# Loading the q of an attention block in one transfer and its k in two, with the whole order of instructions drawn again

## The chip, the cores and the metric

The kernel runs on one core of a Trainium2 chip. The metric is the device time of one execution in microseconds (us). Before the change it is 675.41 us (median of three runs, 675.41 to 675.98).

## What is computed

A transformer block on 2048 tokens (S) of width 448 (D), in float32: layer norm, attention with 16 heads of 28 channels in which each token sees itself and the 255 tokens ahead of it, a residual, layer norm, a GEGLU feed-forward part with 1792 hidden channels, and a residual.

```python
qkv = (x @ wqkv).reshape(B, S, 3, H, Dh)             # H = 16, Dh = 28
scores = einsum("bhqd,bhkd->bhqk", q, k) * Dh ** -0.5
mask = (idx[:, None] - idx[None, :] >= 0) & (idx[:, None] - idx[None, :] < 256)
p = softmax(where(mask, scores, -1e9))
o = einsum("bhqk,bhkd->bhqd", p, v)                  # then @ wo
h = x + A(layernorm(x))
h2 = h + (gelu(n @ w_gate) * (n @ w_up)) @ w_down    # n = layernorm(h)
```

## The kernel before, in words

**Numbers.** Most operands are kept as two or three parts of lower precision, a high part and what is left of it, and a product is a sum of several matmuls over such parts. ScalarE (ACT) writes high parts (L252), VectorE (DVE) or GpSimd (POOL) the low ones (L255), and `mul` (L249) is the one line of nearly all matmuls on TensorE (PE).

**Stages.** First x is loaded in 16 tiles of 128 tokens (L510), normalised, and transposed on PE (L320). `project_tile` makes 128 rows of q or k for a chunk of 512 tokens with eleven matmuls of 512 columns; ACT and DVE split the sum into parts in SBUF, and `put` stores them to DRAM with two DMAs (L656 two parts, L657 one part). The heads form four groups of four (112 channels each); there are two passes p of two groups. The k of the last group is made from 16 rows left over in each of seven tiles, so it goes to DRAM in small pieces (16 rows).

**Attention blocks.** A block B is one group g and one chunk c of 512 tokens: 16 blocks, eight in each pass, c = (B % 8) // 2. `loads(B)` brings q and k back from DRAM in another layout: the 84 rows are 28 channels in three parts, and four heads stand side by side. One tile is 128 tokens of four heads. A block needs four tiles of q, and of k the same four and the two of the chunk ahead (for c = 0 there are none). Each `get` (L678) loads two tiles, 336 KB: a block with c > 0 issues five (k of the chunk ahead, then q, k, q, k), one with c = 0 issues four. The buffers for q and k are two, used by turns (u = B % 2), so a load of block B can be issued only when the matmuls of block B-2 that read the same two tiles have ended.

`scores` multiplies q with k (up to 384 columns) and DVE takes the maximum (L701); `maxima` splits the maxima (DVE L721), transposes them on PE (L728) and has ACT copy them beside q, so that `probs` makes the scores again with the maxima taken off; ACT does exp (L775) and POOL cuts the mask (L788, select). `attend` multiplies with v (L807), `drain` divides by the sums (L830 to L835), `output` multiplies with wo (operands wos, ohl).

**What sets the order.** The program builds a list of operations, each with its engine, costs and a key, and a table PLAN of numbers plays them: it fixes the order on every engine, on SyncE (SP) too, which issues all DMAs in order, and the PSUM banks. A DMA at the head of SP that waits for its data or its buffer holds all behind it. Transposes of `ident` (L1315) fill gaps of PE. The feed-forward part follows from about 306 us on.

Of the kernel before, what the change touches and what calls it, by code (L numbers as in the profile page):

```python
# [135 lines left out]
def block_kernel(ctx: ExitStack, tc, x, wqk_in, wv_in, wo_in, ffn_in, halves_in, out):  # L136
# [499 lines left out]
    def project_tile(p, c, m):  # L636
# [17 lines left out]

        def put(rows, d, name, s, size):
            dma(key, 458 * size, lambda: nc.sync.dma_start(d[:, s:s + 2], both[rows]), tok, [(name, 0)])  # L656
            dma(key, 229 * size, lambda: nc.sync.dma_start(d[:, 2 - 2 * s], both[rows, 0]), tok[0:1], [(name, 1)])  # L657
        put(slice(0, GF), qk_d[g][c][s], ("d", g, s, c), s, 1)
        put(slice(GF, 128), qk_d[NG - 1][c][1][16 * m:16 * m + 16], ("d", NG - 1, 1, c, m), 1, 0.15)
# [8 lines left out]
    def loads(B):  # L668
        g, c = block(B)
        u = B % 2  # L670

        def get(s, cc, lo, n, at, key):
            src = qk_d[g][cc][s].rearrange("(j p) b t -> (p b) j t", j=4)[:, :, lo * 128:(lo + n) * 128]
            dst, tok = (rk, "rk") if s else (rq, "rq")
            rd = [(("d", g, 1, cc, m), i) for m in range(WT) for i in range(2)] if s and g == NG - 1 else \
                [(("d", g, s, cc), i) for i in range(2)]
# [1 line left out]
            dma(key, 246 * n, lambda: nc.sync.dma_start(f(dst[u][0:3 * DH, :, at * 128:(at + n) * 128]), src),  # L678
                rd, [(tok, u, at + i) for i in range(n)])
# [646 lines left out]
    "{i7-vjspMgN*MO#VNOw4-TbdwSR_Z_KlOoOB=B!c{<jt=%o_X8YUr=mAJ+b;6@||v9Nvrnvz!00{_kl5|LzJHRws(oKaM<ycsO$qd8V<jZcyYX"
    "4Obh4D~rQx|LX_C=>9zs{vAQ#)9|11fBXL5{r>lL|Nq7Pzw^T&VT2VY!ipWqNUTWxr-<;?K}wJfq>7l49T*@!hzC-G#2^Yt4|0V5PoFd(CddUc"
    "fM_5GNCq;3v>*iX01qSq=|J-T%*_j;gPb5L$OLkO%Ag9!2daW<zz5Yq4WNLUAT!7hl7bi@%YWvy1_eMH&=#}<?Lh~S6$sD~bOHq<JUWA!unQ;z"
    "x`JAuHmCzk&<)fD^+93K0H~lL2tXsy7&HM*K{L=CXrKis0a}8=U<hahro*8i5s+XQhzo{;5nu+K1((2)U=)}QM}sk78LS7!0t-w5-N8~g6&QFN"
    "=mDmIB49e0180EoU?!La955Tq0TVz^Fc+2urNE>JRCB>{I1$)j9#{ZZz@=arFmW#s4bKP5L2s}EBmjNDLbwRbg9|`$uq0x}N-!U;0xRJ{&=;%*"  # L1330
    "YrrDd4{QS#?hm$u0bnCs1#P?-o&*wS53L1j;U;(*tOEmq3wD6La5Y>HqT|hQAM8!m!9k!H*a>3b^>9B-igtnBz`>`$7PtZK0Y$+9xESmO`@mK>"
    "8SDpZ;5K*woB`XRi(}%xgd-2f!VjT>0(=mDf<E2>Kf|5yAov1z!LP6nsRa6w4d5FbL3YFM@Fd&=AHhT56nqT(lSA+{+z3MWFc4@nh=LEpA8->m"
    "0)N8TxFm>*kHRD12|Na$!ZYw0EDerB6`h4A;B%NBzkui9OL!i>f*0UxcoAL%aquPZ29^UEa7O$K#>bc7d#Ite@G|@jGvO<+JkZfQco|dxFF<B|"
    "1!Rd3{V0+ZR|E#S3a^7~cr?k56W|*l5rpU^_z15-6UD_>!3TI9TBr=T2BM(&Fb9r@ZL}5KfKNa|92Mon(GWs6VJ>_NJ^};CZ5SPmBu~K|h>=8N"
    "$Xyr%Jq85bgE3Jed>_U_x4{E=9t<Q7x&v;4S6~pi0AeE_-2#>I5K;xd1{5X6RdEtLn1oO@TpcHdXTeZ%4lwivxab2IOOAm!s0O|Z-hu?MCLTtT"
    ";#xQ%{0NfaxM&=?2Zj?5b;aXJHyohk_&BJICz2F69-2T>;&&hw?vCT5)c6^A57OWyuntaw(&GDI5=ns4;Vs|+sEeP2qo4<Ff**o}C^P&7GQytt"
    "GZ=}oz@)Gjo=ke<OfV%(jQZeIuqmEGzJO-<8z=y?!oIi&EC|1XemFPIgNwqvI3KQu^W*Oz8*GjX;NPGz{sHRa{+LD_*NM<iP!Q*Xzd%D=2)Drb"
    "VN1+l16&w$SPC}6MX&-PEDc-Xq8LF9o&c?}fI74whBj=2lOq+j#RLXW!ge?WOF$Dwf$gyaU04zp$0cw{Y(Ni|!ck!t+yR%yWpFfD7N>{FkPpk@"
    "@;C#mfQ#W|up&+i3&H5H5>5w;!Opl0EDSs1>@YPPfQ!QzuoEr|hvGD_988JI!yGUL$_XpLTyPj3h%3S2I5!-DW5SWRA{>lI;Z$fU$pc5@)MyMI"
    "f~S#mC@+i!)1bF>I!TYl;@Ge`Ob%PX86+*L569t_a3&dqv!Pj}0jv(QquFE*sS0brxnv&6fvUmzWIWD^YQhDiGR%N#!3j7M%807KqvROLjE<9u"  # L1340
    "xG}5?+rcLA1et`}!z`#C>;O-atf(VAMLNNTuq?`j3Zl`d6>J1^quQ`FJWUFrQRob51J9DqupF9-^PtjbA<2uzpmU@dEQ5-oMPwRYO!A?^s2HjP"
    "myoe&DantDpk-t^X$z;|6=Wr;g$khaWHN3FtDveV4lIsVk=p12NdZ@rlBfi#hN`2uunR1OYM_fG9$Z7}pz^2!>Ix^Iif9~KODdylq#LY@>Y?#y"
    "9l1^_q3&=xzCk9U^<)FNMCzlPWFu*eHjy513Tl8hlP0Jm+CpxTsi+g`infw&Xf?V`x}$Am4Vr|ulRIQGT8eg%IjASROO~P5s0Zqa=AwI~4eAB&"
    "lLw?1+KAes-tZyWg!;gSs5fek+M&Mi5$Ok8plPTkYL6PB{%|@P06U;rs3{r=XQMu7CT@mC!Oo~J8VE<j8Mq%B16!j0=qg!>W}pFR5bT1kkX2|f"
    "90H$_nP@#~g%+c=Xcis{2cmgsEL?(~kmYC?91iEB%VZrI2N$40Xa!n?HlTNOA=-?_!!2k8d`f2HC3q{E0GHy4a68(8R^Y*CCz=Gep?zpSnhaOs"
    "DewTA3U{IBWE#ATmf=Ns2-=NakmdL#*@K3nS7b4MO|GCj=q@^nPNI8gFM30Up*i?1IfmYmxp)CSg$|-a=sj78hocYVH{OUplEdgG+JtwK-S`u^"
    "g?5qMWDj12Z=*frH2O;RlFwux*-y@(tLQPgj}DN7WHo+Icj80jI68t3lWS-f{y{FH6X+-TK!1@V<UHDp&!S7{LBz%5A)1FTphxH&`b{92AMr?f"
    "j3B*%wqQiI;wNZ7Msy9v<T~1hG5tvQ;_Y}Xeu@aCbO&a11X_pp;b(}`19$^Ih(FQw_z+g8MxUd@_&g@$DE>w-V4axc1^P^nVM;FI<M;%AiB4jR"
    "9Ki}P$SHgVpT)1xLu}A<SS6>iO$5~lBd^hQ{EZ0m2&?ohdV?gnf#0F`s3iYRIr)GbqSNT)3%!Y5@&#SOukdSp3&$WI(I@l<U&S8ziaw*u_!@qU"
    "zoD=6Ilh9wqZjxGdV+t@pXew3jb7rI<SzEf9ef|hinwk=Y|#h!Eq;f8A%yQ?lfK9C$!+`rCnO2TM~pGUHhqRaVS*D8jwMy_Q%teIUr1~cmwd)i"  # L1350
    "NgR@xs93}CNI<^eC?pAqMt;!{NlJA5n<gV)aX^!kJuC%DMM5+NO--WFG$bZXN%pd|BnpjA_px*&1Ib9DQitwmnMh8Op13qK@n|lRg&bf$%}(0V"
    "tRyAPO}>+ZEC)$N)6z;L52;M5kaV;vNlr_XYNQPLh7Yk6G!Ffa%aX$^E=^67(!3-MJ;Jh)f+QbFOq0>0tPm+q3XmkUFgeCbkfP)Vu1?C4BBVTt"
    "McdP}tQg5p&av3E9X-z~kPECMEk!P}c=QrG&Mvd~v?95}e&Va_47<iklIyGk%}CSJ8!Q3ML~D?QGy}cO64A^w3q8Sp;hXF<%SvmKTPz>#L9^2w"
    "G(SBV@%VwP7p+CI(NhdD%yQD&q&Foj7p1HK%}smK%9OD#G!NxWVReXLMQIhPvVt@(y~n!JVzdyw&oow&K469EL^_@pr;}(Y`j8c&k5~yhfsUn*"
    "SzS_^j-yrSR9c4ip-<Q}T8~tt<>^z_mp)?^Xhk}i)}$X;C0dI%pylWkI-1s|4QV6Vn2w<XXm$FWHKBFrKw6jfqh)D*@}AYB4M>05jecZJX(!r{"
# [155 lines left out]
```

## Time and profile before

| | |
|---|---|
| median of three runs | 675.41 us |
| the profiled execution's own time | 675.42 us |
| its span in the trace | 673.7 us |
| busy: PE, DVE, ACT, POOL | 662.4, 511.0, 406.9, 325.1 us |
| matmuls in the trace | 4074 |
| loads of q and of k (L678) | 32 and 44, of 336 KB each |
| granted clock of PE | 1.0 |

How to read the views: times are us from the span's start. A row of the timeline or of the chain of waits has the start, the length, and the engine, line and operation; "bank<-ring" is output<-input by the program's names, with numbers left out, and xN says how many instructions are drawn together. SPq is SP issuing a DMA. PEld is the loading of a matmul's weights, which runs beside the matmul ahead of it. In the order of instructions (from the program and not from a run), rows stand in issue order on one engine, with the output's and the input's names and the shape.

### The profile page before, as it was taken

Reading aid. Unit: us, or ns where it says so; the run is one execution under the profiler, and the core shown is the slowest. Engines: PE = TensorE matmul, PEld = TensorE weight load, DVE = VectorE, ACT = ScalarE, POOL = GpSimd, SP = SyncE. Lnnn points to the kernel's source line nnn. Section 1 sums busy time; section 2 is a strip of 40 time slices with the busy share of each in tenths; the row PEclk is TensorE's granted clock in tenths of the full one; section 3 lists DMA queues with packets and bytes.
Section 4 is the critical chain, followed back from the end, with each engine's and each line's share of the span. In section 5 each row is a group of like instructions: output and inputs, shape, how many; then the busy total and the mean of one; then the engine's idle time right before and its main releaser. Section 6 shows DMA issues by size and latency. Waiting matters only on the chain.

```text
span 673.7 us, 12051 instructions
## 1 busy us (share of the span) xinstructions
PE 662.4 (98%) x4074; PEld 591.8 (88%) x4074; DVE 511.0 (76%) x1287; ACT 406.9 (60%) x793; POOL 325.1 (48%) x506
## 2 busy tenths in 40 slices
...
GB/s 296 204 257 234 272 203 180 210 190 196 153 188 212 209 207 227 157 112 86 140 108 102 102 96 119 103 91 93 20 71 53 122 68 119 54 67 55 64 15 109
DMA packets 97814, 93.73 MB, mean 139 GB/s; under 512 B 39064, under 2 KB 86360, under 8 KB 97752
## 3 DMA queue, kind: packets, MB, share of 16 engines
...
q14 instruction: 30, 0.25, 0.1%
...
## 4 chain that ended last, share of the span: by engine, by line
PE 91%; DVE 3%; DMA 2%; SPq 1%; issue 1%; POOL 1%; ACT 1%; DVEq 0%; POOLq 0%
PE bank L249 84%; PE bank L807 6%; DVE bank L701 1%; DMA ring<-k 1%; DMA pp<-in_wv_dram 1%; DMA q<-proj 1%; POOL proj L255 1%; PE bank L320 1%; PE bank L728 0%; DVE mhl L721 0%; ACT pp L775 0%; SPq L657 0%; ACT ring L252 0%; POOL pp L788 0%; SPq L510 0%
## 5 line engine op out<-in xcount | busy, mean ns | idle before, releaser
L249 PE MATMUL bank<-xT,proj 128*128 128x512 f32 x648 | 183.4, 386 | 0.0
L701 DVE CUSTOM_DVE_ANT_0 bank<-bank,mask 128x384 f32<-128x384 f32 (+2 forms) x256 | 131.5, 550 | 23.5 <-PE bank L249 18.4
L249 PE MATMUL bank<-ring 84*128 84x384 f32 (+7 forms) x629 | 140.1, 311 | 1.7 <-DMA ring<-k 0.7
L249 PEld LDWEIGHTS bank<-xT,proj 128*128 128x128 f32 x648 | 118.5, 190 | 12.4 <-issue 0.4
L249 PE MATMUL bank<-xT,ring 128*128 128x512 f32 x508 | 127.5, 379 | 0.0
L249 PE MATMUL bank<-ring,proj 128*128 128x448 f32 x617 | 125.3, 353 | 0.0
L249 PEld LDWEIGHTS bank<-ring,proj 128*128 128x128 f32 x617 | 116.5, 189 | 2.8
L249 PEld LDWEIGHTS bank<-ring 128*128 128x128 f32 (+1 forms) x629 | 106.1, 190 | 12.5 <-ACT pp L775 2.0
L775 ACT ACTIVATE pp<-bank 128x384 f32<-128x384 f32 (+1 forms) x212 | 103.9, 534 | 21.8 <-PE bank L249 18.2
L249 PEld LDWEIGHTS bank<-xT,ring 128*128 128x128 f32 x508 | 95.9, 189 | 12.2 <-DVE v L1022 0.3
L788 POOL TENSOR_SCALAR_AFFINE_SELECT pp<-pp 128x512 f32<-128x512 f32 x120 | 73.3, 639 | 63.1 <-ACT pp L775 61.2
L249 PE MATMUL bank<-proj,xT 128*128 128x224 f32 x352 | 72.6, 268 | 1.1 <-ACT proj L252 1.1
L946 POOL TENSOR_TENSOR raw<-raw 64x128 f32<-64x128 f32 (+1 forms) x110 | 54.9, 510 | 28.7 <-DMA raw<-in_halves_dram 17.1
L249 PEld LDWEIGHTS bank<-proj,xT 128*128 128x128 f32 x352 | 59.4, 191 | 2.3 <-ACT proj L252 1.3
L255 POOL TENSOR_TENSOR ring<-raw,ring 128x256 fp32r<-128x256 f32 (+2 forms) x48 | 43.1, 906 | 35.1 <-ACT ring L252 34.2
L1022 DVE TENSOR_TENSOR v<-v,bank 128x512 f32<-128x512 f32 x48 | 32.8, 683 | 30.6 <-PE bank L249 26.0
L252 ACT ACTIVATE ring<-bank 8x512 fp32r<-8x512 f32 x64 | 37.0, 584 | 24.5 <-PE bank L728 23.6
L255 DVE TENSOR_TENSOR proj<-v,proj 128x512 fp32r<-128x512 f32 (+1 forms) x57 | 38.6, 691 | 17.3 <-ACT proj L252 17.0
L249 PE MATMUL bank<-wos,ohl 128*128 128x448 f32 x192 | 49.3, 359 | 0.1
L252 ACT ACTIVATE proj<-v 128x512 fp32r<-128x512 f32 (+1 forms) x57 | 32.9, 593 | 26.2 <-DVE v L1048 13.6
L1078 DVE TENSOR_TENSOR hres<-bank,hres 128x448 f32<-128x448 f32 x64 | 37.5, 616 | 12.7 <-PE bank L249 12.6
L946 POOL TENSOR_TENSOR v<-raw 128x256 f32<-128x256 f32 x22 | 18.0, 818 | 57.2 <-DMA raw<-in_halves_dram 30.1
...
## 6 DMA issues: line engine op xcount, KB each, us to landing
...
```

What stands on the lines that cost most here:

```text
L249: nc.tensor.matmul(o.rearrange("p (t h) -> p t h", h=2), w, mixed(m), **how)
L252: nc.scalar.activation(dst, src, AF.Copy)
L255: (eng or nc.vector).tensor_sub(dst, src, f(hi))
L320: nc.tensor.transpose(bank[b.k][:, n * 128:(n + 1) * 128], xn[i2][:, o:o + 128], ident)
L701: nc.vector.tensor_tensor_reduce(at, at, plain(mask[:, o:384]), 1.0, -BIG, OP.add, OP.max, mx[i // 2][:, i % 2, j:j + 1])
L775: nc.scalar.activation(pp[:, j:j + per, o * 128:o * 128 + n].rearrange("p j (h t) -> p j h t", h=2), bank[b.k][:, 0:n * per].rearrange("p ...
L788: nc.gpsimd.affine_select(a, a, pattern=[[0, 4], [-cm, 128]], compare_op=op_, fill=0.0, base=0, channel_multiplier=cm)
L807: nc.tensor.matmul(bank[b.k][32 * j:32 * j + DH + 1, lo * 128:(hi + 1) * 128], v[:, 4 * c - 2 + m, g % 2, j, :], pp[:, j, at[m] * 128:(at[ ...
L946: op("pool", 0.14 + n * 0.00215, 0.18 + n * 0.00215, key, lambda: nc.gpsimd.tensor_tensor(out, a, b, op=OP.subtract), [*ar, *br], w, port= ...
L1022: op("dve", 0.605, 0.702, key, lambda: nc.vector.tensor_tensor(plain(out), plain(a), unmixed(bank[bs[i].k]), op=OP.add), ar, w, bs[i])
L1078: op("dve", 0.533, 0.626, key + 3 * q + 3, lambda t=t, b=banks[q]: nc.vector.tensor_tensor(plain(hres[:, t, :]), unmixed(bank[b.k][:, 0:D] ...
```

## The change

In DRAM each group's q and k now is one tile over all 2048 tokens instead of four of 512, so a stored row of two parts falls into two runs of 2 KB where it was one of 4 KB. A block's q is loaded in one transfer of four tiles (672 KB). Its k is loaded, for c > 0, as the first four tiles (672 KB) and the last two (336 KB), and for c = 0 as four at once. That makes 44 loads instead of 76. The whole-q load waits for all of block B-2's matmuls that read that q.

```diff
+LOADS = {2: 492, 4: 560, 6: 760}
+ROWS = (((0, 0, 4, 0), (1, 0, 4, 0)), ((0, 0, 4, 0), (1, -2, 4, 0), (1, 2, 2, 8)))
...
-    qk_d = [[[dram.tile([GF, 3, 512], F32, name=f"{'qk'[i]}{g}_{c}") for i in range(2)] for c in range(CS)]
-            for g in range(NG)]
+    qk_d = [[dram.tile([GF, 3, S], F32, name=f"{'qk'[i]}{g}") for i in range(2)] for g in range(NG)]
...
-            dma(key, 458 * size, lambda: nc.sync.dma_start(d[:, s:s + 2], both[rows]), tok, [(name, 0)])
+            dma(key, 458 * size, lambda: nc.sync.dma_start(d[:, s:s + 2, at], both[rows]), tok, [(name, 0)])
...
-            dma(key, 246 * n, lambda: nc.sync.dma_start(f(dst[u][0:3 * DH, :, at * 128:(at + n) * 128]), src),
+            dma(key, LOADS[n], lambda: nc.sync.dma_start(f(dst[u][0:3 * DH, :, at * 128:(at + n) * 128]), src),
                 rd, [(tok, u, at + i) for i in range(n)])
         key = 16 * B - (8 if B > 1 else 24)
-        if c:
-            get(1, c - 1, 2, 2, 0, key)
-        for i in range(0, 4, 2):
-            get(0, c, i, 2, i, key + 4 * i)
-            get(1, c, i, 2, 2 + i, key + 4 * i)
+        for s, t, n, k in ROWS[c > 0]:
+            get(s, t, n, key + k)
...
 PLAN = (
-    "c-pOZW3+5L)McEV?QGSxZQHhO+qP}nwr$(CZ5w^wx%KY%`cIG1qkGh-IxES_%3O2J<Rl1C00992aKHeHXfc2zY!cazBCLOYQN%cout22EBP|f&"
...
+    "c-pPGW7H+f5-pm}tjaR-Ywosf+qP}nwr$(CZQHhOci%p}zrD}7|K1z#jT);~X5@^Fh#3*Ns>T9<0t5&E00Rd2pBeZ)BELuY_xwLH@MjhMzS!>%"
...
```

The table PLAN is replaced as a whole, so instructions move on every engine up to about 306 us; the feed-forward part keeps its order on PE. The numbers of matmuls, of DVE, ACT and POOL operations stay as they are, but for the transposes of `ident`, which are 33 instead of 30. Lines stand one (matmul, 249 to 250) to seven (load, 678 to 685) further down.

Three places. On SP, the start of the program (hres is x, raw the weights of q and k, pp the weights of v), before:

```order
L510 DMA hres<-in_x_dram 128x448 x4
L583 DMA pp<-in_wv_dram 128x448
L609 DMA raw<-in_wqk_dram 128x512
L583 DMA pp<-in_wv_dram 128x448
L510 DMA hres<-in_x_dram 128x448
L609 DMA raw<-in_wqk_dram 128x512
L510 DMA hres<-in_x_dram 128x448 x10
```

and now:

```order
L511 DMA hres<-in_x_dram 128x448 x3
L584 DMA pp<-in_wv_dram 128x448
L511 DMA hres<-in_x_dram 128x448
L584 DMA pp<-in_wv_dram 128x448
L511 DMA hres<-in_x_dram 128x448 x2
L610 DMA raw<-in_wqk_dram 128x512
L511 DMA hres<-in_x_dram 128x448 x2
L610 DMA raw<-in_wqk_dram 128x512
```

The second load of v's weights is the sixth DMA and was the seventh, with none of the weights of q and k ahead of it; those are the ninth and twelfth and were the sixth and ninth.

On SP, around the loads of block 1, whose q and k are those of group 1, chunk 0 (before q1_0 and k1_0, now q1 and k1; the last number is a buffer's), before:

```order
L657 DMA q1_1_96<-proj_78 112x512
L656 DMA k3_1_113<-proj_78 16x1024
L657 DMA k3_1_113<-proj_78 16x512
L860 DMA raw_79<-in_wo_dram 128x448
L657 DMA k3_1_113<-proj_78 16x512
L657 DMA k3_0_111<-pp_145 16x512
L678 DMA ring_77<-k1_0_95 84x4x256
L678 DMA ring_77<-q1_0_94 84x4x256
```

and now:

```order
L659 DMA k1_89<-pp_121 112x2x512
L660 DMA q0_86<-proj_78 112x512
L685 DMA ring_77<-q1_88 84x4x512
L660 DMA k0_87<-proj_78 112x512
L660 DMA k3_93<-proj_78 16x512
L659 DMA k3_93<-proj_78 16x2x512
L659 DMA q0_86<-proj_78 112x2x512
L685 DMA ring_77<-k1_89 84x4x512
```

The last load of block 1's k was the 55th DMA of the program and is the 44th now; it stood behind stores of chunk 1 of group 1 and of the last group, and stands behind those of chunk 1 of group 0 now.

On PE, in the middle, between the last matmul of block 3 that reads its q (the first row of each piece) and the first scores of block 5 (the last row; ring holds q and k). Rows with xT are of the projection, L728 or L732 is the transpose of the maxima, L807 or L811 the start of block 4's attend. Before:

```order
L249 MATMUL bank7_141<-ring_77 128x384
L249 MATMUL bank3_137<-ring_77 128x384
L249 MATMUL bank1_135<-ring_77 128x128 x2
...
L249 MATMUL bank2_136<-xT_76,proj_78 128x512 x3
L728 MATMUL bank1_135<-one_84,mhl2_150 72x128
L807 MATMUL bank5_139<-pp_145,v_81 29x128 x4
...
L728 MATMUL bank0_134<-one_84,mhl0_148 72x128
L249 MATMUL bank1_135<-ring_77 128x256
L249 MATMUL bank6_140<-ring_77 128x384
```

and now:

```order
L250 MATMUL bank3_113<-ring_77 128x128
L250 MATMUL bank0_110<-xT_76,proj_78 128x512
L250 MATMUL bank7_117<-ring_77 128x384
L250 MATMUL bank6_116<-ring_77 128x384
L250 MATMUL bank1_111<-ring_77 128x384
L250 MATMUL bank0_110<-xT_76,proj_78 128x512 x4
L250 MATMUL bank7_117<-ring_77 128x384
L250 MATMUL bank2_112<-ring_77 128x384
L732 MATMUL bank3_113<-one_84,mhl2_126 72x128
...
L732 MATMUL bank1_111<-one_84,mhl0_124 72x128
L250 MATMUL bank7_117<-ring_77 128x384
```

The 24 matmuls of attend stand between them in both. Beside those there were 21 matmuls from the release of block 3's first two q tiles to the first scores of block 5, and there are 12 now from the release of all four.

More of the change, by code (lines that the diff above doesn't have):

```diff
@@ L652, in project_tile @@
         op("dve", 0.603, 0.698, key, lambda: to_lo(plain(hl[1]), unmixed(bank[b.k]), plain(hl[0])), [tok[0]], [tok[1]], b)
+        at = slice(512 * c, 512 * c + 512)
         def put(rows, d, name, s, size):
[L656 to L659, printed above, removed]
+            dma(key, 458 * size, lambda: nc.sync.dma_start(d[:, s:s + 2, at], both[rows]), tok, [(name, 0)])
+            dma(key, 229 * size, lambda: nc.sync.dma_start(d[:, 2 - 2 * s, at], both[rows, 0]), tok[0:1], [(name, 1)])
+        put(slice(0, GF), qk_d[g][s], ("d", g, s, c), s, 1)
+        put(slice(GF, 128), qk_d[NG - 1][1][16 * m:16 * m + 16], ("d", NG - 1, 1, c, m), 1, 0.15)
     def block(B):
@@ L670, in loads, with get @@
         u = B % 2
-        def get(s, cc, lo, n, at, key):
-            src = qk_d[g][cc][s].rearrange("(j p) b t -> (p b) j t", j=4)[:, :, lo * 128:(lo + n) * 128]
+        def get(s, t, n, key):
+            lo = 4 * c + t
+            src = qk_d[g][s].rearrange("(j p) b t -> (p b) j t", j=4)[:, :, lo * 128:(lo + n) * 128]
             dst, tok = (rk, "rk") if s else (rq, "rq")
-            rd = [(("d", g, 1, cc, m), i) for m in range(WT) for i in range(2)] if s and g == NG - 1 else \
-                [(("d", g, s, cc), i) for i in range(2)]
+            at = t + 2 * s
+            rd = []
+            for cc in range(lo // 4, (lo + n + 3) // 4):
+                rd += [(("d", g, 1, cc, m), i) for m in range(WT) for i in range(2)] if s and g == NG - 1 else \
+                    [(("d", g, s, cc), i) for i in range(2)]
             rd += [("zk" if s else "zq", u, i) for i in range(2)]
-            dma(key, 246 * n, lambda: nc.sync.dma_start(f(dst[u][0:3 * DH, :, at * 128:(at + n) * 128]), src),
+            dma(key, LOADS[n], lambda: nc.sync.dma_start(f(dst[u][0:3 * DH, :, at * 128:(at + n) * 128]), src),
                 rd, [(tok, u, at + i) for i in range(n)])
         key = 16 * B - (8 if B > 1 else 24)
-        if c:
-            get(1, c - 1, 2, 2, 0, key)
-        for i in range(0, 4, 2):
-            get(0, c, i, 2, i, key + 4 * i)
-            get(1, c, i, 2, 2 + i, key + 4 * i)
+        for s, t, n, k in ROWS[c > 0]:
+            get(s, t, n, key + k)
         got[B] = L.ops[-1]
@@ L1326 @@
[L1326 to L1355, printed above, removed]
@@ new lines @@
+    "{=?%x7XJ2tMDoQV?SOx^Q6x|JU+jM~%>Lk5B(wim#D8WaQtO{g{ImLZcHo~p{GI!MVrKti=RY>-pYOl3{ZEB}fA`0cOoGTd<o|lk|IO3i*8jPq"
+    "$egpt8sPtCmHgTNztsjKv&;X@IghmRcOAihndOl+$RjI>{agF!Poyj|OFVK<7HI=Vb`JbEZ~yp2BG*u)?C<+O`TeJ({;mraiG}}D34eFRKR6f}"
+    "E&5l+|K;GH&ip%?|FQ@p{X>ztB7e|-v-?jE!GF68M#hQ%wFDwN?(ca1Bd3uO{=)|N*D8+e{(toU$=yE;!vA4|MauuF*8lp!BTo(#+3g@Qu79}x"
+    "+fNwT{rFFh;y+#VH=g~8lK$Is=zr$;-}CElkN=DNZ&m%%;q>2bg^}z3-R1u)?*F#?|KGm<?{NR&G69J7dldUmrTz5>XMp5DffOL?Z*)o!0kVO3"
+    "APz_c;)0wYM#TS<D>X1dy5H84g7hFa$N<uS0AvSILE?Y)^MGU^2M9r05Ch}|xj;sc@PGEM1fqb-pbDr8@_{6v8mJCxfJ`9sZ$vAQAG8K-KwHob"
@@ new lines @@
+    "2+$sM09imyPypya`@Px`bOHszB-j~r0rfzA&;T?9g+L?F7}Nr_fd%S-CZH*32BLxHU<zyjih$B!5Qq*2gKl6l><*^FAwYtmU>Fz<7Q$)J1tY*n"
+    "FbddUJ{%3kfXQG1q<9J#3lf2;pa<v)7QtSiEa(mTfN7u@=nAHTabO0R4*P<BU?x}$X8{k42mQfp5EIM+b-@7OgBfrFh#s*Oa9kM7hTFh)umkJ_"
+    "GvO{U7YqcuK`F2V%mZ^^MZj=NFbgjJ9oZf*7w!f7z(TMD?gz!ee6SQu0&Cz}xDGA@4p;z|gQ8$PTnbNsd2k|#60riTfE(aOxDp8L;Z1Ne+yXVc"
+    "46XvJfsa?h<!}vH1=oTda3?GQw!&>t$GhNaxDM=wd*Dg17w&`Q!G3rE2KXS9cs*!G?!dcnJG=)&Y~Vw%133bZ!uwF+!|)h94oiX)(84DnMi1Zy"
+    "@DLsVkKkiy;wNw;cnY7vMS!68grZI0AUFk|!_)8#JPa7>NY28(<Q#khIqF32gB#!wxBzT?6TE@~y?_qZ&|4TEyo3FSizD!R_yK-|pWu1;89o3N"
@@ new lines @@
+    "z!&%xUIaRd1ACKiP$C081((1Dco9AWmtZpd9bSf4;6rc@M8QAcd2kt&0p{<c<0`xcf5PkV21F=8QSnXq2qec>z-yQSN5{8dO5BHp=p~GXQ{mM3"
+    "HcW%#LWTO1v^X7xC_TOkGT@hBGdKfc;Eebc_yr@-Sr8LPLFGU!d<}Fa&p~W_9YjUZ&<hX;$Hk{W7jhc>g`=acBnFCyAA{~BKE4GK;BF)#PJ|QV"
+    "*WfL%P$`@QzX7Fj85|EL#ZN#?lmxn{2YCmMfZXsl=t<gO8~La${tFEt?eKe$6t>46>P0%>Sg0d*&>b+4YytN`Y}5(IMP>0_P!4|pd0=@Q4^_ZJ"
+    "NN0Qu#6f9bewYp(1%pTzTmW{(@zF;xl%$29z+F0+RK%6=XHXee!QF6rIE;J)Kfo7I71zeYNgbR4eg$=LEnE-(1od$>Tm%0C-$4VM31@_ve;+Xv"
+    "*2GybhgmU$)p0hAAci@ifZ1^ltU(BKK>~B)TsSvQi1J_^7KIJ535!7s8qk3*Y=mui90ag2mari7U<jMwLQuiHxG9c+J}eCL;RGlO%#RD;BCsGX"
@@ new lines @@
+    "gbU+lI4_I}i{PTT7%q-W;Nq}3P6bQiXs|oZ2V3D1um!$DOTyH!6zqk2;7qU&P6kWE5hOEA0n5TfXe8;2lfzLYC2WoR;WDs4&H_i1mUsZp3gg41"
+    "s5c%%vcbeC8A^_Fz_BC&9Eg*kaik|6PqM>CurW-52H^>0B549^!RRm{9E>Z$+HeT204u}vXcEbYD#8qCD6Rr0lVLa$N{On%dT=<70aKyWs6H$Q"
+    "caSt_Cn*o>z+EIQstc>ZmarA90n?$@a0K2>s>8u37it4*!aZapjtTdYwy-H|2KSN7C^y<q2BGHg0Lh2O;w-2bDuP<TAt);<jt-J3BpVuyr;>JX"
+    "8YzmVlNn?t$&T`%{HOt(MP`#ZWG=~z=8;3BAuNmLlN{(TSPfN2he<h92o*p%QF#;#RzSx{dsrCNKx1%0GzwQlB~T(*62*o`NM$q>l|n~J6?Bpe"
+    "Lkmb%lo&1~i^yWq0WKj+Noh114M)q!a#99$ge%BOG6t<8bx<dGimWCh&}mW^wL@n}dvum`M4e#=)CzS%Bhez%8l5Af(0S4sH9?Ef1u_|Rffvao"
@@ new lines @@
+    "G6gk7&Cndw6<#LIQ7tqVtw7!271AB9L_J__)Du=h4bWB63${QF(L~e*jYTa{Z#W6nLp9M5I24XU<8gg747NpG(Qw!Yc0;pJBQzd$M+?vd)C2W}"
+    "ZBRcr4);X;;X*V5-XtU8Y&077LKE;9xD1Vg^Uw*>7%f2q;8b*-4209rSU3pYAk$HAG#JiA$H_Ia6wN@((R{QDtww#&T)YO2gX_^cG!xIm8_;;T"
+    "74=1H(Ka*-Pk<XyKXi*sgxk?=vI$Mcv+-thhs?lt$tg4kPsI1gX>=J)!h6ttas};0%kWhEfLuk(@k4R|O~X6TPV|TzM32c6vI}j%Ysew=lx)On"
+    "$$Y#UT|gJnVYH4c!0X8tw1HegXV6CSjBFz7@L9B(Y$4asKC~X+qg%-_bOOC5`_UV6pMJ#K$VoIAza>Y|c5)p}!SBd%bOXI7N6}5R5Pu-I&?0;e"
+    "eI)(S2Yef?!JF_Zd>(zmYw;&C0DUH3$Yy*8eI+aKYP<yxM2qoV^o?xA59rF@4{=NJHvF9|!Q1gedJpZukLYK-6Ys`P=@EPs-$#gi!F%v?vg`Ll"
@@ new lines @@
+    "$^*0)@53($CdcqWd<g#_knG3T@Jm9-L-Z3L#$WL(asYqFzwje;22*k!|G-bsWAvClMbFSTY?HJ2IXZzI@{BTa4j;!a5GSwENqir_MCb7n`T)N{"
+    "m+(V;3co^c(F^(xUB>T`Ab0RD@|>Q=cd<)u;CuKA)`&+wpbPjDLi8s7j6R|-=pw#~zoO{mF^)<e;TYrz4#`s-L2hA1p5brkCxY}jjz)f=+rJ-S"
+    "F@^XgjY1H9fq#<k2xF7{Kt9pQOB@h`SVWST<S#<-D;kTu!f}Z~W0QD9(D=lpt63ak(F9}-)96~3kR&EHO+s|Kj=jc7Nivd%NSd4wx}K#VX$Yl^"
+    "rXp#{2F7Vh5{srIsmVqbo4&#EXnInV6eBTdd|I58Ae-1<)T1RyK9Zlrp+4Qr3Xlw>6p2ft(=99`$wFe#s5BeNN-~kHEE>&4vXdO-EzV2|l0qam"
+    "sZSlchvg*o=w9a1eXKCq&+?E1ETHf3L3W6Rv<OK=x3L8DFw0Ahu!Qs|JI1y%MN5<8EHRCsXIK)Nlt!Tq=zDyEon*UMGFpbbrs-)4x|?O7Z|Gb4"
```

193 lines of the change are left out of this document (96 added, 97 removed).

## The prediction, on record before the run

> **What bounds the kernel now.** I read the page first, then the windows of 20 us, the waits of PE, the chain of waits, and last the timeline around single loads. The page says how much is to be had: PE is busy nearly throughout, and the chain that ended last is PE's.
>
> ```profile
> PE 662.4 (98%) x4074; PEld 591.8 (88%) x4074; DVE 511.0 (76%) x1287; ACT 406.9 (60%) x793; POOL 325.1 (48%) x506
> PE 91%; DVE 3%; DMA 2%; SPq 1%; issue 1%; POOL 1%; ACT 1%; DVEq 0%; POOLq 0%
> ```
>
> 673.7 less 662.4 leaves 11.3 us without a matmul in flight. The windows (length, then busy time of PE, PEld, DVE, ACT, POOL, granted clock, DMA share, GB/s) say where:
>
> ```profile
> 0.00:20.00 20.00, 16.28 (x101) 14.88 (x102) 14.79 (x33) 10.63 (x18) 12.70 (x31) 1.00 0.76 259
> 40.00:60.00 20.00, 19.34 (x126) 17.51 (x125) 18.20 (x67) 15.25 (x29) 2.50 (x5) 1.00 0.79 245
> 100.00:120.00 20.00, 19.52 (x148) 16.30 (x146) 18.10 (x60) 15.90 (x33) 10.15 (x14) 1.00 0.63 180
> 160.00:180.00 20.00, 19.38 (x158) 17.09 (x157) 16.05 (x58) 13.96 (x27) 9.45 (x12) 1.00 0.39 115
> 280.00:300.00 20.00, 19.69 (x142) 16.23 (x141) 17.30 (x54) 15.50 (x35) 10.96 (x18) 1.00 0.46 109
> 320.00:673.70 353.70, 348.85 (x1698) 320.32 (x1696) 244.94 (x465) 175.25 (x332) 158.66 (x250) 1.00 0.29 84
> ```
>
> 3.7 us are idle in the first 20 us and 4.85 after 320 us; the rest, 2.7 us, is spread over the attention part. The clock is 1.00 in every row, so no time is to be had from it. The feed-forward part is one piece of the chain, and its order is not touched:
>
> ```profile
> 306.15 362.71 PE bank L249 x1764
> ```
>
> So only what PE waits for before 306 us can change. Its waits in the attention part (engine, line, what it waited for: us in total, times, longest):
>
> ```profile
> PE bank L728 <- DVE mhl L721: 1.0, 3, 0.6
> PE bank L249 <- DMA ring<-k: 0.7, 1, 0.7
> ...
> PEld bank L249 <- ACT pp L775: 2.2, 9, 0.6
> PEld bank L249 <- DVE mx L701: 1.8, 7, 0.5
> PEld bank L249 <- DMA ring<-k: 0.4, 1, 0.4
> ```
>
> Together 6.1 us, some of it overlapped by a matmul still running. Loads of q and k cost 1.1 us of this, at two places:
>
> ```profile
> 54.90 0.46 PE L249 MATMUL bank<-ring 84*128 84x256 f32 x2 [0.66 <-DMA ring<-k]
> ...
> 69.46 0.19 PEld L249 LDWEIGHTS bank<-ring 84*128 84x128 f32 x1 [0.43 <-DMA ring<-k]
> ```
>
> The first is block 1, the second block 2; the loads of the other blocks arrive before PE needs them. Taking away 32 loads therefore saves PE nothing by itself. What can move the time is where each load stands, and the new order around it.
>
> **The change part by part. The start: -0.35 us.** The first matmuls with v's weights wait for the second load of these:
>
> ```profile
> 3.13 0.43 SPq L609
> 3.61 5.54 DMA pp<-in_wv_dram
> 9.17 0.59 ACT proj L252
> 9.80 1.03 PE bank L249 x7
> ...
> 13.24 6.65 PE bank L249 x41
> ```
>
> The row at 3.13 is the load of 256 KB of other weights that the new order puts behind. At 259 GB/s (the window of the first 20 us) 262 kB take 1.0 us, so v's weights can land 1.0 us earlier and PE can start at 8.8. That is the gain if nothing else holds PE; but from 13.24 on PE is busy with v and the projections, and those need the transposed x, which DVE and ACT make tile by tile, and the weights of q and k, which now come three DMAs later. They bound the gain at -0.9, and at +0.1 if the later weights hold the first projection. I take a third, -0.35.
>
> **Block 1's k: -0.6 us.** This is the longer of the two waits. SP's rows ahead of it:
>
> ```profile
> 43.93 0.30 SPq L656 DMA_DIRECT2D k<-proj  x1
> 44.28 0.43 SPq L657 DMA_DIRECT2D k<-proj  x1
> ...
> 49.07 0.41 SPq L678 DMA_DIRECT2D ring<-k  x1
> 49.53 0.43 SPq L678 DMA_DIRECT2D ring<-q  x1
> ```
>
> ```profile
> 49.07 5.70 DMA ring<-k
> 54.90 1.66 PE bank L249 x8
> ```
>
> The load was issued at 49.07, behind five stores and a load of weights (the order above, in the change), and landed 5.7 us later. In the new order it stands behind stores of chunk 1 of group 0, which went out by 44.28, so it can go some 5 us earlier. But the first scores of block 1 are earlier too: they were the 325th matmul and are the 302nd, at 362.71 / 1764 = 0.206 us each 4.7 us. The margin thus improves by a few tenths only from the order, and by what the wait for fewer stores ahead saves (5.70 is the longest flight on the chain; less traffic makes it shorter). Bounds, block 2's wait included, which goes if its loads are released in time: -1.1 (no wait left) and 0 (as now); I take half, -0.6.
>
> **The whole-q load: +0.5 us.** A load of block B waits for the matmuls of block B-2 that read its buffer. SP already stands in this wait, which costs nothing as long as the load still lands in time:
>
> ```profile
> SPq L678 <- PE bank L249: 59.4, 30, 6.7
> ```
>
> Before, half of q could go when the first two tiles were free; now all of it waits for the last. The rows of PE show it at block 5: 21 matmuls and attend stood between release and first scores, and now it is 12. Attend has its row:
>
> ```profile
> 126.94 2.73 PE bank L807 x48
> ```
>
> So there is 2.73 us and twelve matmuls at between 0.1 (the small ones) and 0.206, with a mean of about 0.19: 5.0 us of room. Counted the same way, the tight blocks have 5.0 (block 5), 5.1 (6), 5.6 (4 and 12) and 5.8 (2); the others 6.6 or more. The k loads keep 7 or more. How long a load of 672 KB takes no row shows; the nearest are these. The first tile of x, 224 KB on empty queues, and block 6's first loads, k and q of 336 KB each, issued 0.19 and 0.56 us after the release at 123.11:
>
> ```profile
> 0.79 1.82 SPq L510 DMA_DIRECT2D hres<-in_x_dram  x4
> ...
> 3.24 0.63 DVE L285 BATCH_NORM_STATS2 bnst<-hres 128x6 f32<-128x448 f32 x1 [1.26 <-DMA hres<-in_x_dram]
> ```
>
> ```profile
> 123.11 0.54 PE L249 MATMUL bank<-wos,ohl 128*128 128x448 f32 x2
> ...
> 123.30 0.33 SPq L678 DMA_DIRECT2D ring<-k  x1
> ...
> 123.67 1.33 SPq L678 DMA_DIRECT2D ring<-q  x2
> ...
> 129.60 0.43 PE L249 MATMUL bank<-ring 84*128 84x384 f32 x1
> ```
>
> ```profile
> 122.00:130.00 8.00, 8.00 (x81) 6.37 (x80) 7.66 (x24) 4.21 (x9) 4.09 (x6) 1.00 0.79 230
> ```
>
> The first gives 2.45 us, and 448 KB more at 230 GB/s another 2.0: 4.4 us. The second gives the other end: PE did not wait at 129.60, so two loads, together 672 KB, had landed within 6.5 us of the release, with stores around them. A four-tile load with the k load ahead of it by 0 to 2.7 us lies between, at 4.4 to 6.5; I take 5.1 and 0.2 for the issue, 5.3 us after the release, nearer to the quiet end since k's bytes are mostly through. That leaves 0.3 us to wait in block 5 and 0.2 in block 6: +0.5, with ends 0 and (1.5 + 1.4 + 2 x 0.9 + 0.7) = +5.4.
>
> Here the Trainium skill says less: in "DMA: Bandwidth & Descriptors", section "Anatomy of one DMA", a DMA (there issued from GpSimd) costs about 2.0 us plus its bytes at 436 GB/s. By that 672 KB take 3.6 us, an estimate, and the term would be 0, the sum 0.5 lower; but the same rule gives 2.8 us for the load at 49.07 that took 5.70, so under this traffic the trace disagrees.
>
> **The stores: 0.** A two-part store now writes runs of 2 KB, not 4. Nobody but a later load waits for them, and 14 of 16 blocks had their loads in time. The cover gone, it would show in the loads as above.
>
> **The rest of the new order: -0.75 us.** The waits for ACT and DVE above (1.0 + 2.2 + 1.8 us) hang on how many matmuls stand between a step and its use. Two are long enough to name:
>
> ```profile
> 169.12 1.19 DVE mhl L721
> ```
>
> ```profile
> 298.82 0.50 ACT pp L775
> 299.37 3.95 PE bank L249 x15
> ```
>
> At 298 PE waits for exp after exp of block 15, whose last matmuls of probs stand bunched; in the new order projections stand between them, so I take 0.5 of that off. DVE's step at 169.12 took 1.19 us where its like at 268.64 takes 0.51:
>
> ```profile
> 268.64 0.51 DVE mhl L721
> ```
>
> Such a hold can fall on another block, so I take 0.25 for the rows that have more room and count it as uncertain. Bounds: -2.0 (the named waits gone) and +1.5 (the new order has as many and one or two longer ones).
>
> **The sum** is -0.35 - 0.6 + 0.5 - 0.75 = -1.2 us against the profiled execution's own 675.42, which stands 0.01 above the median of 675.41. That gives **674.2 us**. About 0.2%, 1.35 us, is what a measurement of this kernel can tell from no change, so the forecast lies just inside that bound.
>
> **The rivals.** *Slower: the whole-q load is late.* SP cannot issue it before the last matmul of block B-2 that reads q, and each tight block then waits. It decides from a landing 5.6 us after the release, when four blocks are past their room. With the 5.70 us of block 1's row and 0.2 to 0.6 of issue, 6.3 us, the waits are 1.3 + 1.2 + 0.7 + 0.7 + 0.5 = 4.4 in place of 0.5: 674.2 + 3.9 = 678.1. For it speaks that 5.70 is a measured flight of half the bytes; against it that this load had five stores and a load of weights just ahead, and that 672 KB came within 6.5 us in block 6, which is one of the tight ones. Chance 0.14.
>
> *No change: stalls trade places.* The first 20 us are bound by DVE and ACT, block 1's k and scores move up alike, and the waits for exp and maxima come back elsewhere: -0.3, 675.1. For it speaks that all these waits together are small and scattered and that no work goes from PE. Chance 0.24.
>
> *More: nearly all of it goes.* The load waits vanish, the start gains 0.9, and of the waits for ACT and DVE 2.0 go, while the q loads come in time: -0.9 - 1.1 - 2.0 = -4.0 at most; I price it at three quarters, -3.0: 672.4. For it speaks that 32 issues and their traffic go from a busy queue (the DMA share is 0.6 to 0.8 up to 160 us). Chance 0.14.
>
> **How the numbers follow.** The forecast has 0.48, with a range of its own from 673.2 to 675.2. Of it 0.29 lies more than 1.35 us below the 675.41, where the search for an order had more freedom than I credit, and 0.19 within. Faster: 0.29 + 0.14 = 0.43; within 0.2%: 0.19 + 0.24 = 0.43; slower: 0.14. The range takes in the three cases that are not slower, and goes up to 3.0 us above the forecast, which q loads that land 6.0 us after the release would give (1.0 + 0.9 + 2 x 0.4 + 0.2 = 2.9, not 0.5), with half a us for the start: 671.6 to 677.2. The slower case's own middle, 0.14, is left out.
>
> **What would show it right or wrong.** The first matmul with v's weights before 9.3 us and the first projections earlier than now show the start. No wait of PE for ring<-k near 49 us shows block 1; 0.4 us or more there shows half of it kept. Waits of PE or PEld for ring<-q at the first scores of blocks 5 and 6, 0.2 to 0.3 us each, show the price of the whole load; none at all, or more than 1 us, shows the term wrong. Fewer than 2.2 us of waits for ACT pp, and none at the end of block 15, show the last term. The prediction is wrong if the piece of the chain behind 306 us changes its length of 362.7, or if the time leaves the range.

## The result, and the profile after

The changed kernel takes **714.49 us** (median of four runs, 714.11 to 722.87) against 675.48 us: a ratio of 1.0605, interval 1.0528 to 1.0683. It is 39 us slower. The prediction said 674.2, in a range of 671.6 to 677.2, and gave "slower" a chance of 0.14. The ratios further down leave out two disturbed executions, one of 695.0 us (only q halved) and one of 3920.4 us (the old order with the new layout), which is the profiled one, so no trace of that version is read.

The page of the profile after, its busy line and its chain:

```profile
PE 677.4 (95%) x4077; PEld 605.6 (85%) x4077; DVE 513.1 (72%) x1287; ACT 406.6 (57%) x793; POOL 324.4 (46%) x506
PE 74%; DMA 18%; DVE 4%; SPq 2%; issue 1%; ACT 0%; DVEq 0%; ACTq 0%
```

The span is 712.9 us where it was 673.7, so 39.2 longer. Two things make that up. PE is without a matmul for 712.9 - 677.4 = 35.5 us where it was 11.3: 24.2 more. And PE is busy 677.4 - 662.4 = 15.0 us longer with the same matmuls (three small transposes aside). DMA, 2% of the chain before, is 18% now. The windows show both (columns as before; the granted clock is the third number from the end):

```profile
0.00:20.00 20.00, 17.31 (x109) 15.75 (x110) 15.69 (x33) 10.08 (x15) 14.08 (x33) 1.00 0.74 248
...
100.00:120.00 20.00, 18.04 (x145) 15.27 (x147) 14.63 (x46) 11.93 (x24) 7.01 (x10) 0.91 0.52 143
120.00:140.00 20.00, 17.43 (x126) 15.04 (x122) 15.74 (x50) 12.26 (x25) 7.38 (x11) 0.83 0.69 199
...
160.00:180.00 20.00, 16.74 (x126) 14.49 (x127) 13.20 (x45) 10.41 (x22) 6.28 (x10) 0.92 0.68 203
```

PE was idle 0.6 us or less in these windows after the first; now it is idle 2.0 to 3.3 us, and the clock, 1.00 in every row before, is 0.83 to 0.92 in the three shown. The feed-forward part is not to blame: from the end of the last attend on PE is busy 362.8 of 367.4 us, where it was 362.7 of 367.6. PE's waits say for what:

```profile
PE bank L250 <- DMA ring<-q: 20.0, 10, 2.7
...
PE bank L250 <- DMA ring<-k: 5.0, 4, 2.5
PEld bank L250 <- DMA ring<-q: 2.7, 1, 2.7
...
PEld bank L250 <- ACT pp L779: 0.6, 2, 0.4
```

27.7 us of waits for loads, where there were 1.1; PE's weight loads wait 0.6 us for exp, where they waited 2.2. Block after block reads like block 6. First its loads at SP, then the chain, then PE:

```profile
134.99 0.32 SPq L685 DMA_DIRECT2D ring<-k  x1
136.99 0.31 SPq L685 DMA_DIRECT2D ring<-q  x1
```

```profile
136.99 7.29 DMA ring<-q
144.28 0.14 issue
144.41 8.02 PE bank L250 x48
152.44 8.01 DMA ring<-q
...
168.36 9.08 DMA ring<-q
```

```profile
144.41 0.74 PE L250 MATMUL bank<-ring 84*128 84x384 f32 x4 [2.45 <-DMA ring<-q]
```

The whole q flies 7.29 us and PE stands still for 2.45 of them; the next two fly 8.01 and 9.08.

### The profile page after: what moved, and what is told of

Same layout as the page of the kernel before. It is cut to its first block, busy times and chain, and to the rows that moved or that the text cites. A ratio compares the mean times of both kernels' runs of the same rounds, so it can differ in the third digit from the quotient of the medians.

```text
span 712.9 us, 12003 instructions
## 1 busy us (share of the span) xinstructions
PE 677.4 (95%) x4077; PEld 605.6 (85%) x4077; DVE 513.1 (72%) x1287; ACT 406.6 (57%) x793; POOL 324.4 (46%) x506
## 4 chain that ended last, share of the span: by engine, by line
PE 74%; DMA 18%; DVE 4%; SPq 2%; issue 1%; ACT 0%; DVEq 0%; ACTq 0%
PE bank L250 72%; DMA ring<-q 11%; DMA ring<-k 3%; DMA k<-proj 2%; PE bank L811 1%; DVE X L256 1%; DMA raw<-in_ffn_dram 1%; SPq L367 1%; DMA hres<-in_x_dram 1%; DVE v L467 1%; DVE proj L256 1%; DVE xT L256 1%; SPq L660 1%; DMA v<-xn 0%; PE bank L321 0%
## 5 line engine op out<-in xcount | busy, mean ns | idle before, releaser
L250 PE MATMUL bank<-xT,proj 128*128 128x512 f32 x648 | 179.2, 386 | 0.0
L250 PE MATMUL bank<-ring 84*128 84x384 f32 (+6 forms) x629 | 145.1, 326 | 27.7 <-DMA ring<-q 20.0
L250 PEld LDWEIGHTS bank<-ring 128*128 128x128 f32 (+1 forms) x629 | 113.1, 204 | 39.4 <-issue 25.2
L250 PE MATMUL bank<-proj,xT 128*128 128x224 f32 x352 | 60.5, 275 | 0.5 <-DVE xT L256 0.5
L250 PEld LDWEIGHTS bank<-proj,xT 128*128 128x128 f32 x352 | 55.8, 195 | 2.4 <-ACT xT L253 0.7
L250 PE MATMUL bank<-wos,ohl 128*128 128x448 f32 x192 | 54.6, 395 | 0.0
L256 DVE TENSOR_TENSOR proj<-v,proj 128x512 fp32r<-128x512 f32 (+1 forms) x57 | 36.9, 664 | 17.4 <-ACT proj L253 17.0
L250 PE MATMUL bank<-X,ring 128*128 128x512 f32 x138 | 45.5, 379 | 0.0
```

Source lines behind the costliest of these rows:

```text
L250: nc.tensor.matmul(o.rearrange("p (t h) -> p t h", h=2), w, mixed(m), **how)
L256: (eng or nc.vector).tensor_sub(dst, src, f(hi))
```

## The experiments

Each run stands beside its own runs of the kernel before on the same chip (medians 674.15 to 675.14), and each ratio is to those. The theories: **flight** (a load of four tiles lands late, and all at once), **order** (the new order leaves too little room), **layout** (rows 8 KB apart in DRAM are slow), and **clock** (part of the loss is matmuls at half clock after a wait).

**Both loads halved.** The four tiles go as two DMAs of two, at the same place of the new order:

```diff
+            def bring():
+                for i in range(0, n, 2):
+                    nc.sync.dma_start(f(dst[u][0:3 * DH, :, (at + i) * 128:(at + i + 2) * 128]),
+                                      src[:, :, i * 128:(i + 2) * 128])
```

> Each load of four tiles is issued as two DMAs of two tiles, one behind the other, at the same place of the new order and in the new layout. Flight theory (a load of 672 KB in runs of 2 KB flies 5.5 us alone and 7 to 9 us behind another, longer than the room of 5 to 7 us): the first half lands some 3 us after its issue and the second 4 to 4.5, waits of PE for ring<-q and ring<-k fall from 27.7 us to under 6, the granted clock comes back to 0.99 or more, 676 to 684 us. Order theory (the new order leaves too little room for any load that waits for the last matmul of block B-2): the waits stay over 15 us and the time over 700 us. Layout theory (reading rows that lie 8 KB apart in DRAM is slow): the halves fly 5 us or more as well, and the time stays over 700 us.

Measured: 679.94 us, ratio 1.0067 (1.0043 to 1.0092). The flight theory's 676 to 684 holds. Order and layout are those of the changed kernel, and 34 of its 39 us are gone, and the slow clock with them: PE is busy 662.6 us again. That speaks against the layout. Against the order it is no full test, since a half of two tiles also has a release of its own and need not wait for the last matmul of block B-2; the halves by heads and the old order below are to decide that.

```profile
PE 662.6 (98%) x4077; PEld 593.2 (87%) x4077; DVE 510.6 (75%) x1287; ACT 405.9 (60%) x793; POOL 324.5 (48%) x506
```

```profile
PE bank L250 <- DMA ring<-k: 2.6, 2, 2.1
PE bank L250 <- DMA ring<-q: 2.0, 1, 2.0
```

**Halved by heads.** Two DMAs of two heads each, so that the runs stay at 2 KB:

```diff
+                w = 2 if n == 4 else 4
+                for i in range(0, 4, w):
+                    nc.sync.dma_start(f(dst[u][0:3 * DH, i:i + w, at * 128:(at + n) * 128]), src[:, i:i + w])
```

> Each load of four tiles is issued as two DMAs, of two heads each, so that the runs stay at 2 KB and only the size of a DMA is halved. If the run of 2 KB is what is slow, the second half lands as late as the whole load does now (5.5 us after the issue, or later behind another), while the first scores, which read the first heads only, start after the first half, some 4 us after the issue: 685 to 705 us. If it is the size of the single DMA, the second half lands within 4.5 us as in the kernel with two tiles a load and the time is that kernel's, within 3 us.

Measured: 689.98 us, ratio 1.0243 (1.0215 to 1.0270): within the 685 to 705 us of the first branch, but not for its reason, the run of 2 KB, as the flights show (issue to the last engine's completion in the trace, us; "alone" means that nothing of size was ahead):

```text
load                                             kernel           flights
336 KB, two tiles, alone                         both halved      3.0 to 3.2, once 4.4
336 KB, two tiles, 0.4 behind another            both halved      4.2 to 5.2
336 KB, two heads, alone                         by heads         3.2 to 3.9
the second two heads, 0.4 behind the first       by heads         4.4 to 5.2
672 KB, four tiles, alone                        changed          5.5 to 5.9
672 KB, four tiles, 0.4 behind another 672 KB    changed          8.0 to 9.1
672 KB, four tiles, 1.3 to 2.0 behind another    changed          7.2 to 8.1
```

A run of 2 KB is not what is slow: 336 KB in such runs fly hardly longer than in runs of 1 KB. Two halves are there 4.6 to 5.6 us after the first one's issue, one transfer of the same bytes 5.5 to 5.9: little more. What the single transfer loses is its first half, which lands after 3 us and is all of q that the first scores need (of k they read three tiles, for c > 0 the second half too). By heads the two DMAs still share one release, that of the last tile; by tiles each has its own: the first k of block 7 is issued at 139.55 and 140.09 us by heads, at 134.06 and 139.10 by tiles. So of the 34.6 us between the changed kernel and both halved, 24.5 come with landing in two pieces (714.49 to 689.98). The other 10.0 (to 679.94) go with the release by halves as far as these traces tell; the length of the runs and the part of q and k that lands first differ too, so this share is argued and not shown.

**Padded rows.** The layout theory by itself:

```diff
-    qk_d = [[dram.tile([GF, 3, S], F32, name=f"{'qk'[i]}{g}") for i in range(2)] for g in range(NG)]
+    qk_d = [[dram.tile([GF, 3, S + 64], F32, name=f"{'qk'[i]}{g}") for i in range(2)] for g in range(NG)]
```

> The rows of q and k in DRAM are padded from 2048 to 2112 numbers, so they lie 8448 bytes apart instead of 8192; nothing else is changed. Layout theory: the loads of 672 KB fly 4.5 us or less alone and the time falls under 690 us. Flight and order theory: no change, 711 to 718 us.

Measured: 712.25 us, ratio 1.0579 (1.0534 to 1.0623). No change against the changed kernel's 1.0605, as the flight and the order theory had it; the layout theory's 690 us or less is out.

**The old order with the new layout alone.** Stores and loads address one tile for each group; nothing else is changed:

```diff
-            dma(key, 458 * size, lambda: nc.sync.dma_start(d[:, s:s + 2], both[rows]), tok, [(name, 0)])
+            dma(key, 458 * size, lambda: nc.sync.dma_start(d[:, s:s + 2, at], both[rows]), tok, [(name, 0)])
...
-            src = qk_d[g][cc][s].rearrange("(j p) b t -> (p b) j t", j=4)[:, :, lo * 128:(lo + n) * 128]
+            src = qk_d[g][s].rearrange("(j p) b t -> (p b) j t", j=4)[:, :, (4 * cc + lo) * 128:(4 * cc + lo + n) * 128]
```

> The kernel before with only the new layout in DRAM: one tile for each group's q and k, stores in runs of 2 KB, loads of two tiles in runs of 1 KB from rows 8 KB apart, order and number of DMAs as before. Flight theory: the layout costs nothing, 673.5 to 677 us. Layout theory: every load is slower, over 680 us.

Measured: 675.28 us, ratio 1.0017 (1.0006 to 1.0029). The layout costs about 1 us, and is not the cause.

**The old order with q in one transfer.** The earlier of the two loads issues nothing, the later one brings all four tiles; `w` is 4 here:

```diff
+                half.setdefault(B, set()).add(at)
+                if len(half[B]) == 2:
+                    whole = qk_d[g][cc][s].rearrange("(j p) b t -> (p b) j t", j=4)
+                    for i in range(0, 4, w):
+                        t = slice(i * 128, (i + w) * 128)
+                        nc.sync.dma_start(f(dst[u][0:3 * DH, :, t]), whole[:, :, t])
```

> The kernel before, with its order and layout, but q of a block goes in one transfer of four tiles, at the place of the later of its two loads; the earlier one issues nothing. Flight theory (a transfer of four tiles lands all at once, 4.9 us or more after its issue, where the first of two small ones lands after 3): the first scores stand 4 to 6 us behind the issue in most blocks, so PE waits 1 to 3 us in ten or more blocks and loses clock: 690 to 712 us. Order theory (the loss belongs to the new order): 674 to 680 us.

Measured: 715.56 us, ratio 1.0603 (1.0562 to 1.0645). In the old order one whole q alone costs as much as the change does, 3.6 us more than I had expected at most. The order theory, with 674 to 680, falls.

```profile
PE 678.7 (95%) x4074; PEld 606.6 (85%) x4074; DVE 511.1 (71%) x1287; ACT 407.8 (57%) x793; POOL 325.9 (45%) x506
```

Its whole q's fly as long as those of the changed kernel, for example:

```profile
130.64 5.70 DMA ring<-q
147.11 6.87 DMA ring<-q
```

**The same place, two halves.** `w` is 2 in the code above.

> As the kernel with the whole q in the old order, but the four tiles go as two transfers of two tiles, one right behind the other at the same late place. This tells the size of the transfer from its late release. Flight theory: the first half lands 3 to 4 us after the issue, and waits are a third or less of those with the whole transfer: 676 to 688 us, at least 8 us under the whole one. If it is the late release alone that costs: within 3 us of the kernel with the whole q.

Measured: 690.35 us, ratio 1.0218 (1.0180 to 1.0255), 2 us over what I had expected.

```profile
PE 667.3 (97%) x4074; PEld 595.7 (86%) x4074; DVE 510.1 (74%) x1287; ACT 407.6 (59%) x793; POOL 325.3 (47%) x506
```

```profile
PE bank L249 <- DMA ring<-q: 10.4, 3, 5.6
```

So the late place costs 15 us in the old order, 10.4 of it in three blocks, whose second load of q stood late; the single transfer at the same place costs 25 us more. The two profiled executions lie 27.6 us apart in span (716.9 and 689.3): 11.4 of that is PE's busy time (678.7 - 667.3) and 16.2 idle time.

**Only q halved, only k halved.** Both in the changed kernel; in the first one, `w` is n for k and 2 for q, in the second the other way round:

```diff
+                for i in range(0, n, w):
+                    nc.sync.dma_start(f(dst[u][0:3 * DH, :, (at + i) * 128:(at + i + w) * 128]),
+                                      src[:, :, i * 128:(i + w) * 128])
```

> The changed kernel, its k whole as changed, only q's load issued as two of two tiles. The first scores need all that is ahead of them in the queues: k's 672 KB and half of q. Bytes at some 250 GB/s: the first half of q lands 1.3 us earlier than the whole q does now, so of the 25 us of waits about 10 stay, and half of the loss of clock: 690 to 700 us. If q alone is what is late: 680 us, as with both halved.

> The changed kernel, its q whole as changed, only k's loads of four tiles issued as two of two. The bytes ahead of the first scores are the same as in the changed kernel, 1344 KB, and q still lands at once: the waits for ring<-q stay within 5 us of 20 and the time is 705 to 715 us. If the whole k ahead is what makes q late: under 695 us.

Measured: 685.87 us with q halved (1.0159, 1.0106 to 1.0211), 691.09 with k halved (1.0236, 1.0205 to 1.0267). Both of my expectations were too high: with q halved I had 690 to 700, with k halved 705 or more, and the other branch there, under 695 if the whole k ahead is what makes q late, is the one that came out. Either halving alone takes off most of the 39 us, so it is the two whole loads one behind the other that cost, and not q's alone. PE's waits with k halved:

```profile
PE bank L250 <- DMA ring<-q: 6.2, 5, 2.1
PE bank L250 <- DMA ring<-k: 3.5, 3, 1.7
```

I had reckoned with the same bytes ahead of q. But a half has a release of its own: in block 7 the first half of k leaves at 135.27 and the second at 141.33, with q at 141.73.

```profile
135.27 0.31 SPq L688 DMA_DIRECT2D ring<-k  x1
...
141.33 0.31 SPq L688 DMA_DIRECT2D ring<-k  x1
141.73 0.39 SPq L688 DMA_DIRECT2D ring<-q  x1
```

So only one half still stands ahead of q, which flies 5.4 to 7.4 us in blocks 2 to 8 instead of 7.2 to 9.1. Merged, both halves wait for the later release, and q queues behind all of it.

**Filled waits.** Transposes of the identity, which need no load, ahead of the first scores of each block from the third on; 24 of them, and 15 in a second run:

```diff
+            if B > 1 and B not in met:
+                met.add(B)
+                for _ in range(24):
+                    warm(b.k)
```

> 24 transposes of the identity are put on PE ahead of the first scores of each block from the third on; they need no load, and take about 2.6 us where they find a wait. Clock theory (of the 39 us, 24 are idle time of PE and 15 are matmuls at half clock after each wait): the waits for the loads are filled, the granted clock is 0.99 or more, and the time falls by 10 to 15 us, to 700 to 705, although work is added. If the clock falls for another reason than idle time: the clock stays at 0.98 and the time is 714 us or more.

> The changed kernel with 15 transposes of the identity, some 1.6 us, ahead of the first scores of each block from the third on: fewer than the 24 of the run before, so that they fit into the waits of 2 us each, and shorten what is left to below half a us. Clock theory: the clock stays full, nearly all the added work lies in waits, and the 15 us of slow matmuls go: 697 to 704 us. If the waits and not the clock carry all of the 39 us: 711 us or more.

Measured: 712.84 us with 24 (1.0570, 1.0548 to 1.0591), 703.59 with 15 (1.0436, 1.0420 to 1.0452). With 24 the clock is full but the time is in neither range that I had given: the added work, 698.0 - 662.6 = 35.4 us, is longer than the waits, 27.7 us. With 15 it is 686.0 - 662.6 = 23.4 us, the clock is full too, and the time is in the range:

```profile
PE 686.0 (98%) x4287; PEld 615.0 (88%) x4287; DVE 510.7 (73%) x1287; ACT 406.4 (58%) x793; POOL 324.4 (46%) x506
```

11 us go by adding work that nothing reads. Work in a wait can save nothing but the clock, so at least 11 of the 39 us are the clock's price. It is less than the 15 us of slow matmuls because the filling is not free: PE's idle time falls from 35.5 to 16.2 us, by 19.3, so some 4 of the 23.4 us added lay in no wait.

**The start alone.** In the kernel before, the sixth and seventh DMA change places:

```diff
+        at = [i for i in range(len(banks), len(words)) if words[i] < n and self.ops[words[i]].eng == "sp"]
+        words[at[5]], words[at[6]] = words[at[6]], words[at[5]]
```

> The kernel before with one change at its start: the second load of v's weights is issued ahead of the first load of q's and k's weights, the swap that the new order makes there. The prediction took 0.35 us for it, with ends at 0.9 less and 0.1 more. If DVE's transposed x and the later weights hold the start all the same: within 0.2 us of the kernel before.

Measured: 674.26 us, ratio 0.9998 (0.9988 to 1.0008): no change that can be told. The interval, -0.8 to +0.5 us, takes in both nothing and the 0.35. The first projections start at 14.61 instead of 15.07, and in the one trace this lead is not lost: the same matmuls stay at least 0.46 us ahead of those of the trace before, and the feed-forward part starts 1.3 us earlier than at 306.15. Most of the difference between 0.46 and 1.3 is block 1's wait of 0.66, which this trace does not have.

```profile
304.85 362.79 PE bank L251 x1764
```

## Why the prediction was wrong

**The start (-0.35).** The size was about right where I looked: the first projections start at 14.65, 0.42 earlier. The other sign failed, the first matmul with v's weights before 9.3: it stands at 9.51 (9.80 before) and waits for DVE, as the bound had it.

```profile
9.51 0.67 PE L250 MATMUL bank<-proj,xT 128*128 128x224 f32 x4 [0.49 <-DVE xT L256]
```

```profile
14.65 0.61 PE L250 MATMUL bank<-xT,proj 128*128 128x512 f32 x2
```

Whether such a gain reaches the end is not settled by the swap alone: its trace keeps the lead, its times cannot tell it from nothing. In the changed kernel the waits for q cover it.

**Block 1's k (-0.6).** The load left 6 us earlier, at 43.08, as worked out. But it flew until 50.8, 7.7 us, and PE waited 1.22 us instead of 0.66 (the row names a store that landed after it; the load is what the scores read):

```profile
51.06 0.29 PE L250 MATMUL bank<-ring 84*128 84x128 f32 x1 [1.22 <-DMA k<-proj]
```

**The whole-q load (+0.5): the step that failed.** The prediction put a four-tile load "between, at 4.4 to 6.5; I take 5.1", "nearer to the quiet end since k's bytes are mostly through". Three things were wrong in this one step. First, the flight alone: 5.5 to 5.9, not 4.4 at the quiet end, where I had added 448 KB at the mean rate of a busy window to the flight of a small load. Second, k's bytes were not through. The lead was as I had counted it, up to 2.7 us: SP issued k 0.4 to 2.6 us ahead of q in blocks 2 to 8 (134.99 and 136.99 above). But k's first load is a whole one now, which alone needs 5.5 us, so most of it was still to come when q was issued. Before the first scores 1344 KB had to land, where my upper end of 6.5 came from 672 KB. Third, that end was itself two loads of 336 KB, with the second two tiles of q in a load behind them that the first scores do not need; a row of two small loads does not bound one large one. The load, put at 5.3 us after the release, landed 7.5 us after it in block 6, and the term of +0.5 measured 22.7 us of waits for q, with k's 5.0 and the clock on top. The room was counted rightly: in block 6 the load landed 7.29 + 0.19 us after the release and PE waited 2.45, which makes 5.03 of room against my 5.1.

**The clock.** The prediction read "1.00 in every row, so no time is to be had from it". That is so for a gain; it left out that time can be lost there. The idle stretch at 103 us, 2.0 us long, in windows of 1 us (PE's busy time, granted clock, DMA share, GB/s):

```profile
104.00:105.00 1.00, 0.00 (x0) 1.00 0.98 241
105.00:106.00 1.00, 0.92 (x4) 0.64 0.95 285
106.00:107.00 1.00, 1.00 (x5) 0.50 0.92 348
107.00:108.00 1.00, 1.00 (x6) 0.50 0.52 201
108.00:109.00 1.00, 1.00 (x6) 0.65 0.00 0
109.00:110.00 1.00, 1.00 (x7) 1.00 0.00 0
```

3.4 us at half clock follow, 1.7 us lost. A wait of two microseconds can so cost nearly twice its length; the filled waits show at least 11 of the 39 us to come from there.

**The slower rival** named the right mechanism and priced it at 678.1. It took 6.3 us for the landing from the one flight of 5.70 and found 4.4 us in five blocks; measured are flights of 7.2 to 9.1 for q in blocks 2 to 8, 27.7 us of waits in 15 places, and the clock on top. The chance of 0.14 rested on "672 KB came within 6.5 us in block 6", the wrong comparison again.

**The stores (0)** and the layout: about 1 us by the old order with the new layout. **The rest of the new order (-0.75)**: the waits for exp fell from 2.2 to 0.6 us, but every block now starts late, so this says little. With both loads halved the new order is 4.5 us slower than the old one. How much of that is the order and how much the late release of q's first half is not settled. No version that was run beats the kernel before.
